# A recurrent matrix-memory layer with an MLP behind it: wider matmul tiles, wider fillers and a new hand-written order on one Trainium2 core

## The chip, the core and the metric

One NeuronCore of a Trainium2 chip runs the whole program. It has a matrix engine (TensorE, PE in the profile, with its weight loads shown apart as PEld), a vector engine (VectorE, DVE), an activation engine (ScalarE, ACT), a general engine (GpSimd, POOL), and a queue that only issues transfers here (SyncE, SP). The metric is the time on the device of one execution, in microseconds (us); lower is better.

## The reference, cut to what matters

```python
# B=4 batches, H=8 heads, S=768 steps, D=40
for t in range(S):                                   # per batch and head
    m_new = max(f[t] + m, i[t])
    f_s, i_s = exp(f[t] + m - m_new), exp(i[t] - m_new);  m = m_new
    C = f_s * C + i_s * outer(v[t], k[t])            # 40 x 40 memory
    n = f_s * n + i_s * k[t]
    y[t] = sigmoid(o[t]) * (C @ q[t]) / max(abs(n @ q[t]), 1)
x  = y, heads side by side                           # (B, S, 320)
xn = (x - mean(x)) / sqrt(var(x) + 1e-6) * g_ln
out = x + max(xn @ w_ch1, 0) @ w_ch2                 # 320 -> 1280 -> 320
```

## The kernel before, in words

**Steps.** The sequence is cut into 6 chunks of 128 rows; a chunk of one batch is a step, so there are 24 steps, numbered `st`, four to a chunk. Two steps side by side make a pair `p` (12 of them), and the MLP works on pairs. In a step, `S` makes the scores of all heads (keys against queries), `ex` makes the decay weights with exponentials, `P` multiplies scores by weights, `int` adds what the memory of earlier chunks gives (it has matmuls from step 4 on), `pv` multiplies by the values, `km`/`kv` make the update of the memory and `sd`/`st` apply it. `n1` to `n3`, `sq` and `np` normalise the row, `T`, `xh`, `xl` transpose it and split it into a high and a low part. `G`/`sel` and `eg`/`qm` bring in the decays of later chunks from DRAM; in chunk 0 (steps 0 to 3) `gx` makes them with matmuls. The pieces that begin with `g` (`gm`, `gg`, `gate`, `gu`, `gta`, `gca`, ...) are the gates of a chunk: scans on VectorE, short rows on GpSimd, two transposes.

**MLP.** `m1.p.f.i` is 8 matmuls of 256 columns (high and low parts of weights and rows), `hh`/`hl` apply the ReLU and split the result, `m2.p.f.j` is 6 matmuls of 320 columns, `ob` adds the input row, `out` stores it. A pair has ten `m1` and ten `m2`.

**Weights.** They come as 64-bit floats, in 11 chunks (`wl.0` to `wl.10`, through 4 buffers), and the kernel turns them into a high and a low 32-bit part: `cA` (ScalarE, absolute value), `cX` (clamp from below, GpSimd), `cT.0` to `cT.2` (VectorE, bit operations), `cH` (ScalarE), `cL` (GpSimd), and four copies `cR`. The first pair needs all of them.

**Order.** Nothing is planned at run time: the string `ORDER` (lines 40 to 129) lists every piece, and each engine, and SP for the transfers, takes its instructions in that order. `@` gives the banks of the matmuls' memory. `fill.n` is a matmul whose result nobody reads. On TensorE every recorded matmul has a weight load in front; a product of 32-bit floats makes two of such pairs (a transpose one). So `S` and `int` make 64 recorded instructions, `pv` 128, `kv` 64, `m1` 16, `m2` 12, `T` 6, `gx` 36, and `fill.128` 2.

The lines that are spoken of later are 363 to 373 (`S`), 413 to 425 (`kv`), 445 to 457 (`pv`), 614 to 617 (`cX`, with the strings `CX` in line 35 and `BUFS` in line 37), 620 to 634 (`cT`), 683 to 691 (`ini`) and 693 to 695 (`fill`).

Of the kernel before, what the change touches and what calls it, by code (L numbers as in the profile page):

```python
# [47 lines left out]
gate.1 fill.128 fill.128 ex.1.0 fill.128 fill.128 fill.128 fill.128 fill.128 gu.1 gst.1 fill.128 fill.128 fill.128
fill.128 fill.128 fill.128 fill.128 fill.128 fill.128 fill.128 fill.128 fill.128 fill.128 gex.1 S.0@4@5 cH.0 gse.1
gm.2 wl.3 fill.128 ex.1.1 gta.1@7 cL.0 cR.0 fill.128 fill.128 P.0.0 fill.128 fill.128 fill.128 fill.128 cR.1 fill.128  # L50
fill.128 fill.128 fill.128 fill.128 fill.128 fill.128 P.0.1 fill.128 fill.128 sig.0 S.1@4@6 gca.1 gr.1 km.1 cR.3
fill.128 cR.2 gtr.1@7 km.0 fill.128 P.1.1 wl.4 kv.1@5 cA.1 fill.128 gg.2 P.1.0 pv.0 st.1 gcr.1 kv.0@6 n1.0 pv.1 st.0
n2.0 cX.1 S.2@4@5 n3.0 ld.4 fill.128 gx.2@0@6 cA.2 cT.1.0 n1.1 fill.128 sq.0 T.0@7 cT.1.1 cX.2 fill.128 fill.128
fill.128 fill.128 ex.2.0 fill.128 fill.128 fill.128 fill.128 fill.128 fill.128 n2.1 fill.128 fill.128 np.0 fill.128
fill.128 fill.128 fill.128 cT.2.0 gx.3@1@2 tok.2 ex.2.1 P.2.0 fill.128 cT.2.1 int.3@3@4 fill.128 fill.128 fill.128
fill.128 km.3 sig.1 fill.128 fill.128 fill.128 fill.128 fill.128 fill.128 fill.128 fill.128 fill.128 fill.128 P.2.1
ex.3.0 km.2 kv.3@0 fill.128 cT.1.2 int.2@5@6 pv.2 G.4 ex.3.1 cT.2.2 eg.2 kv.2@1 fill.128 fill.128 fill.128 fill.128
fill.128 n1.2 fill.128 fill.128 fill.128 G.5 fill.128 n3.1 fill.128 cH.2 fill.128 fill.128 fill.128 fill.128 fill.128
fill.128 fill.128 fill.128 fill.128 fill.128 fill.128 fill.128 fill.128 cH.1 fill.128 fill.128 cL.2 fill.128 fill.128
fill.128 fill.128 fill.128 fill.128 ld.5 fill.128 fill.128 xh.0 n2.2 T.1@2 st.2 fill.128 gate.2 S.3@5@6 st.3 xl.0  # L60
gst.2 xh.1 cL.1 cA.3 fill.128 n3.2 fill.128 fill.128 fill.128 fill.128 fill.128 fill.128 fill.128 sq.1 fill.128
fill.128 fill.128 fill.128 fill.128 fill.128 fill.128 gex.2 fill.128 fill.128 fill.128 fill.128 cX.3 wl.5 fill.128
fill.128 fill.128 fill.128 fill.128 fill.128 P.3.1 wl.6 T.2@7 sq.2 np.1 fill.128 fill.128 gse.2 fill.128 fill.128 cA.4
P.3.0 fill.128 fill.128 fill.128 fill.128 fill.128 fill.128 fill.128 np.2 fill.128 fill.128 fill.128 cT.3.0 xh.2 pv.3
xl.1 cX.4 fill.128 ld.6 S.4@0@1 cT.3.1 gu.2 G.6 fill.128 cT.4.0 m1.0.0.0@6 cT.3.2 cT.4.1 fill.128 cH.3 m1.0.0.1 eg.3
cL.3 n1.3 sig.2 gta.2@5 cT.4.2 fill.128 fill.128 fill.128 fill.128 fill.128 fill.128 fill.128 fill.128 hh.0.0 fill.128
fill.128 fill.128 n2.3 km.4 m1.0.1.0@2 wl.7 cH.4 xl.2 km.5 gr.2 n3.3 kv.4@3 tok.3 fill.128 cL.4 kv.5@7 m1.0.1.1 hl.0.0
sq.3 fill.128 gca.2 T.3@4 sel.4 wl.8 gm.3 hh.0.1 m2.0.0.0@6 xh.3 hl.0.1 sel.5 m2.0.0.1@5 ex.4.1 xl.3 m2.0.1.1 np.3
ex.4.0 P.4.1 S.5@2@4 qm.4 ex.5.0 P.4.0 fill.128 gtr.2@1 fill.128 qm.5 cA.5 m2.0.1.0 P.5.0 ex.5.1 gcr.2 m1.1.0.0@0 cX.5
P.5.1 gg.3 int.4@1@2 cA.6 G.7 cT.5.0 fill.128 pv.4 cT.5.1 fill.128 cX.6 m1.1.0.1 sd.4 cT.5.2 ld.8 cT.6.0 cH.5  # L70
m1.1.1.0@4 st.4 hh.1.0 cT.6.1 cL.5 m1.1.1.1 ld.7 n1.4 cT.6.2 sel.6 m1.0.2.0@3 wl.9 hh.1.1 n2.4 cH.6 m1.0.2.1 hl.1.1
qm.6 ex.6.0 n3.4 int.5@1@2 cL.6 cA.7 pv.5 hh.0.2 sd.5 hl.1.0 m1.1.2.0@4 sq.4 st.5 ex.6.1 cX.7 wl.10 hl.0.2 np.4
m2.1.0.0@7 cT.7.0 n1.5 ld.9 sig.3 km.6 cT.7.1 m2.0.2.0 km.7 n2.5 kv.6@0 cT.7.2 kv.7@3 n3.5 m2.0.2.1 cH.7 cA.8 cL.7
S.6@1@2 eg.4 gate.3 sq.5 gst.3 gex.3 sel.7 m2.1.1.0 gse.3 P.6.0 P.6.1 cX.8 m1.0.3.0@1 ex.7.0 np.5 cT.8.0 m1.0.3.1
ex.7.1 cT.8.1 G.8 gu.3 tok.4 m2.1.0.1@2 hh.0.3 cT.8.2 m2.1.1.1 qm.7 hl.0.3 cH.8 gm.4 m1.1.2.1 cA.9 cL.8 m1.1.3.0@1
hh.1.2 hl.1.2 m1.1.3.1 cA.10 cX.9 cX.10 m2.0.3.0 cT.9.0 hh.1.3 cT.9.1 gg.4 m2.0.3.1 cT.10.0 cT.9.2 m2.1.2.1 cT.10.1
cH.9 m2.1.2.0 cL.9 hl.1.3 gta.3@4 cT.10.2 gr.3 m2.1.3.0 G.9 sel.8 gca.3 gate.4 cH.10 m1.0.4.0@1 gst.4 gex.4 gu.4
ex.8.0 gse.4 m1.0.4.1 ex.8.1 m1.1.4.0@4 cL.10 gm.5 m1.1.4.1 hh.0.4 ld.11 sig.4 hl.0.4 m2.1.3.1 km.9 hh.1.4 sel.9
hl.1.4 T.4@1 m2.0.4.0 xh.4 km.8 ex.9.1 xl.4 m2.0.4.1 gg.5 ob.0.0 ex.9.0 S.7@1@4 ob.0.1 out.0.0 out.0.1 int.6@5@6
gate.5 pv.6 P.7.0 gex.5 gst.5 qm.8 gse.5 sd.6 m2.1.4.1 P.7.1 G.11 n1.6 st.6 S.8@1@4 n2.6 ob.1.1 n3.6 int.7@5@6 out.1.1  # L80
pv.7 ld.10 qm.9 T.5@0 sd.7 sq.6 P.8.1 eg.6 T.6@2 m2.1.4.0 xh.5 np.6 st.7 xh.6 P.8.0 sel.11 int.8@3@4 xl.6 pv.8 ob.1.0
ex.11.0 n1.7 kv.9@1 out.1.0 xl.5 kv.8@2 ex.11.1 gtr.3@7 sd.8 m1.2.1.0@0 gu.5 n2.7 st.8 tok.5 n3.7 m1.2.1.1 m1.2.3.0@5
# [676 lines left out]
```

## Time and profile before

| | us |
|---|---|
| median of 3 runs | 371.09 |
| lowest, highest | 367.81, 372.40 |
| the execution that was profiled, its own time | 370.03 |
| its span, from the first to the last instruction | 368.3 |
| TensorE busy in it (91%) | 334.1 |
| VectorE busy (56%) | 208.1 |
| ScalarE busy (39%) | 144.8 |
| GpSimd busy (37%) | 136.1 |

What the trace says is of the one profiled execution; its own time lies 1.7 us above its span, and 1.06 us under the median of the runs. A busy share is a mean over stages with different limits, so a stretch has to be read by itself. The page of the profile names, for every idle moment, what ended it; "issue" stands where the profile shows nothing that the engine waited for.

### The profile page before, as it was taken

How to read it: one execution, taken by the hardware profiler on the slowest of the kernel's cores; microseconds unless marked ns; L12 is line 12 of the kernel's file. 1: busy time of each engine (PE TensorE's matmuls, PEld its weight loads, DVE VectorE, ACT ScalarE, POOL GpSimd, SP SyncE). 2: the span in 40 equal slices, each digit the busy share in tenths (PEclk: the TensorE clock that was granted, in tenths of full speed). 3: DMA queues.
4: the chain of work that ended last, by engine and by line, in shares of the span. 5: the costliest groups of instructions: out<-in, count | busy, mean ns of one | idle time of the engine just before them, and what ended most of it. 6: DMA issues, size and time to landing. Idle time of an engine off the chain costs nothing.

```text
span 368.3 us, 12884 instructions
## 1 busy us (share of the span) xinstructions
PE 334.1 (91%) x5664; PEld 317.5 (86%) x5664; DVE 208.1 (56%) x475; ACT 144.8 (39%) x374; POOL 136.1 (37%) x169
## 2 busy tenths in 40 slices
...
GB/s 198 302 263 261 226 236 329 81 183 131 136 52 185 248 165 89 118 219 74 159 245 128 117 189 24 28 117 175 189 262 70 17 4 0 2 72 3 0 2 71
DMA packets 15956, 49.42 MB, mean 134 GB/s; under 512 B 1916, under 2 KB 5532, under 8 KB 15900
## 3 DMA queue, kind: packets, MB, share of 16 engines
...
q8 instruction: 44, 0.72, 0.8%
q14 instruction: 12, 0.10, 0.1%
HBM read 43.84 MB, written 4.10 MB: 130 GB/s over the span
## 4 chain that ended last, share of the span: by engine, by line
PE 75%; DVE 8%; issue 7%; POOL 6%; ACT 2%; DMA 1%; SPq 0%; POOLq 0%; DVEq 0%; ACTq 0%
PE banks L550 29%; PE banks L577 9%; PE banks L579 8%; PE banks L578 8%; PE banks L371 5%; PE banks L694 4%; PE banks L454 4%; POOL wt L617 3%; PE banks L407 2%; PE banks L421 2%; PE banks L355 1%; PE banks L516 1%; ACT w L340 1%; DVE y L486 1%; DVE wt L627 1%
## 5 line engine op out<-in xcount | busy, mean ns | idle before, releaser
L562 DVE SCALAR_TENSOR_TENSOR hl<-banks,hh 128x512 fp32r<-128x512 f32 x60 | 41.1, 687 | 77.7 <-ACT hh L555 77.7
L577 PE MATMUL banks<-w2h,hh 128*128 128x320 f32 x240 | 76.8, 320 | 2.2 <-DVE state L442 2.0
L579 PE MATMUL banks<-w2h,hl 128*128 128x320 f32 x240 | 75.0, 313 | 2.2 <-DVE hl L562 2.2
L578 PE MATMUL banks<-w2l,hh 128*128 128x320 f32 x240 | 74.8, 312 | 0.0
L555 ACT ACTIVATE hh<-banks 128x512 fp32r<-128x512 f32 x60 | 35.6, 596 | 92.0 <-PE banks L550 87.4
L550 PE MATMUL banks<-xh,w1h 128*128 128x256 f32 x360 | 66.8, 295 | 0.5 <-DVE w L378 0.4
L550 PE MATMUL banks<-xh,w1l 128*128 128x256 f32 x360 | 64.5, 289 | 2.8 <-issue 2.5
L550 PEld LDWEIGHTS banks<-xh,w1l 128*128 128x128 f32 x360 | 53.2, 196 | 3.3 <-issue 2.7
L550 PEld LDWEIGHTS banks<-xh,w1h 128*128 128x128 f32 x360 | 54.0, 197 | 1.6 <-ACT gg L288 0.7
L340 ACT ACTIVATE w<-w,ar_sb 128x128 f32<-128x128 f32 x160 | 48.9, 390 | 5.4 <-POOL w L329 4.7
L550 PE MATMUL banks<-xl,w1h 128*128 128x256 f32 x240 | 49.1, 287 | 0.0
L577 PEld LDWEIGHTS banks<-w2h,hh 128*128 128x128 f32 x240 | 45.4, 189 | 3.3 <-DVE state L442 2.2
L579 PEld LDWEIGHTS banks<-w2h,hl 128*128 128x128 f32 x240 | 45.5, 190 | 2.5 <-DVE hl L562 2.5
L578 PEld LDWEIGHTS banks<-w2l,hh 128*128 128x128 f32 x240 | 45.6, 190 | 0.1
L384 POOL TENSOR_TENSOR qe<-qk,eg 104x512 f32<-104x512 f32 x20 | 26.4, 1329 | 40.7 <-PE banks L407 19.5
L378 DVE TENSOR_TENSOR w<-banks,w 128x512 f32<-128x512 f32 x48 | 31.5, 684 | 16.7 <-ACT w L340 7.3
L504 POOL TENSOR_SCALAR rs<-rs 128x1 f32<-128x1 f32 x24 | 6.0, 252 | 88.8 <-ACT junk L498 87.8
L550 PEld LDWEIGHTS banks<-xl,w1h 128*128 128x128 f32 x240 | 38.0, 194 | 0.0
L498 ACT ACTIVATE junk<-y,sum 128x320 bf16<-128x320 f32 x24 | 13.5, 561 | 41.6 <-DVE sum L489 41.5
L454 PEld LDWEIGHTS banks<-tok,w 128*32 128x32 f32 x1536 | 17.4, 112 | 12.6 <-issue 11.8
L329 POOL TENSOR_SCALAR_AFFINE_SELECT w<-w 128x1024 f32<-128x1024 f32 x20 | 23.7, 1190 | 9.5 <-DMA w<-gsc 7.2
L371 PE MATMUL banks<-qk 40*64 40x128 f32 x768 | 27.0, 281 | 0.1
...
## 6 DMA issues: line engine op xcount, KB each, us to landing
...
```

The costliest lines, as they stand in the source:

```text
L329: nc.gpsimd.affine_select(out=w, in_=w, pattern=[[0, H], [1, C]], compare_op=ALU.is_ge, fill=NEG, base=0, channel_multiplier=-1)
L340: nc.scalar.activation(out=w[:, h], in_=ps[:, hh], func=AF.Exp, bias=ar_sb[:, c, 0, b * H + h:b * H + h + 1])
L371: nc.tensor.matmul(s_t[st, z][m, g], t[r, 1, g, m], t[r, 0, g], start=True, stop=True, skip_group_check=True)
L378: nc.vector.tensor_tensor(out=w, in0=s_t.pop((st, half)), in1=w, op=ALU.mult)
L384: nc.gpsimd.tensor_tensor(out=t, in0=qk_t[st][:, 0], in1=eg_t[p][:, j], op=ALU.mult)
L454: nc.tensor.matmul(Y[m, h], w[:, h, m], tok_t[p][:, j, h * VA:(h + 1) * VA], start=(c == 0), stop=(c == 0 or g == 3), skip_group_check=True,)
L550: nc.tensor.matmul(ps[:, i], a, x, start=(n == 0), stop=(n == len(ops) - 1))
L555: nc.scalar.activation(out=t, in_=h1_t[p, f], func=AF.Relu)
L562: nc.vector.scalar_tensor_tensor(out=l.rearrange("p a t -> p (a t)"), in0=ps.rearrange("p a t -> p (a t)"), scalar=0.0, in1=t.rearrange("p ...
L577: nc.tensor.matmul(ps, t[:, i, sl], w2h[:, ff], start=(ff == 0), stop=False)
L578: nc.tensor.matmul(ps, t[:, i, sl], w2l[:, ff], start=False, stop=False)
L579: nc.tensor.matmul(ps, l[:, i, sl], w2h[:, ff], start=False, stop=(ff == KF - 1))
```

## The change

Four edits. `S`, `kv` and `pv` of the first four steps (`NE = 4`) use tiles twice as wide (128 instead of 64 columns of weights in `S`, 64 instead of 32 in `kv` and `pv`), so these pieces have half as many matmuls there; later steps keep theirs. The 245 fillers of 128 columns become 18 of 512 columns (`fill.512`) and 4 products of 32-bit floats on 512 columns (`fill.513`, two pairs each). The clamp `cX` of all 11 chunks goes from GpSimd to VectorE. And `ORDER` is written anew: four chunks of weights (3, 2, 0, 1) are loaded and turned ahead of the first scores, the steps of chunk 0 run as 1, 0, 2, 3, and of the later steps `int`, `kv` and `pv` lie further apart, with `m1` and `m2` between. The buffers of `w` and `qk` become 5 each. The diff, with the order cut to its head on both sides and to the surroundings of steps 14 (before) and 10 (after):

```diff
 UMIN = 2.0 ** -15
 
 GP = 4
-CX = "ppppppppppp"
+NE = 4
+CX = "ddddddddddd"
 CL = "ppppppppppp"
-BUFS = {'y': 7, 'xt': 2, 'ht': 4, 'wraw': 4, 'w': 4, 'qk': 4}
+BUFS = {'y': 7, 'xt': 2, 'ht': 4, 'wraw': 4, 'w': 5, 'qk': 5}
 
 ORDER = """
-int.0@0@1 ini id g0 int.1@2@3 wl.0 gin ld.1 fill.128 fill.128 cst fill.128 fill.128 fill.128 fill.128 fill.128
-fill.128 fill.128 ld.0 fill.128 fill.128 fill.128 fill.128 fill.128 fill.128 fill.128 tok.0 fill.128 fill.128 fill.128
-fill.128 gm.0 fill.128 fill.128 fill.128 wl.1 fill.128 fill.128 fill.128 fill.128 fill.128 fill.128 gg.0 fill.128
-fill.128 fill.128 fill.128 fill.128 fill.128 fill.128 fill.128 fill.128 fill.128 fill.128 fill.128 fill.128 gate.0
...
-S.14@2@3 gr.4 gca.4 ob.4.1 ex.17.1 S.16@4@6 out.4.1 P.14.0 ld.18 ex.17.0 int.15@0@1 P.14.1 m2.4.2.0 sd.15 ex.16.0
-m2.4.3.0 ex.16.1 P.16.0 m2.4.4.0 P.16.1 S.15@2@7 ob.4.0 eg.8 S.17@3@4 P.15.1 out.4.0 int.14@5@6 P.15.0 pv.14 P.17.0
-sd.14 pv.15 P.17.1 kv.15@7 n1.14 kv.14@2 n2.14 m1.6.0.0@3 st.15 qm.16 n3.14 gtr.4@4 m1.5.1.0@5 qm.17 n1.15 sq.14 eg.9
-gcr.4 int.16@6@7 n2.15 st.14 km.16 int.17@0@1 n3.15 pv.17 np.14 kv.16@4 km.17 sd.17 pv.16 sq.15 ld.19 n1.17 sd.16
...
+int.1@0@1 ini id g0 int.0@2@3 gin wl.3 wl.2 fill.513 gm.0 gg.0 ld.1 gate.0 wl.0 gu.0 gx.1@4@5 wl.1 gm.1 cA.3 gg.1 cX.3
+gta.0@6 fill.512 cT.3.0 fill.512 gr.0 gca.0 cT.3.1 gtr.0@6 ex.1.0 fill.512 fill.512 fill.512 gcr.0 gate.1 cT.3.2
+ex.1.1 gu.1 gst.1 gx.2@4@6 cA.2 gm.2 gta.1@5 fill.513 gex.1 ex.2.0 gse.1 gca.1 gg.2 cX.2 fill.512 cT.2.0 ex.2.1
+gx.0@4@5 cT.2.1 tok.0 ld.0 cA.0 cT.2.2 fill.513 cH.3 cX.0 fill.512 cT.0.0 ex.0.0 cL.3 fill.512 ld.2 fill.512 cT.0.1
+cH.2 S.1@4@6 cT.0.2 ex.0.1 cL.2 fill.512 fill.512 P.1.0 fill.512 ld.3 cA.1 P.1.1 gx.3@4@5 cH.0 cX.1 cT.1.0 km.1 sig.0
+cT.1.1 pv.1 km.0 ex.3.0 gate.2 cst cT.1.2 gu.2 gst.2 kv.1@6 gr.1 n1.1 kv.0@4 gex.2 n2.1 G.5 cH.1 gse.2 S.0@0@1 cL.0
+gm.3 st.1 st.0 ex.3.1 S.2@4@6 tok.1 P.0.0 cL.1 P.0.1 gta.2@0 cR.0 gtr.1@5 gr.2 gca.2 P.2.1 pv.0 gg.3 n3.1 ld.5 S.3@0@1
+cR.2 fill.512 P.2.0 sq.1 sel.5 gtr.2@6 gate.3 fill.513 P.3.1 gex.3 gst.3 gu.3 ex.5.0 gse.3 fill.512 gcr.2 n1.0
+fill.512 P.3.0 fill.512 G.4 ex.5.1 n2.0 int.2@0@1 np.1 gta.3@4 ld.4 fill.512 gm.4 int.3@2@3 fill.512 gr.3 gca.3 gg.4
+gcr.1 n3.0 gtr.3@6 pv.3 sig.1 pv.2 gcr.3 km.2 sq.0 gate.4 n1.3 gst.4 gex.4 km.3 T.0@4 n2.3 eg.2 T.1@5 n1.2 kv.2@6 gu.4
+xh.0 n2.2 gse.4 xh.1 xl.0 kv.3@2 st.2 S.5@0@3 xl.1 st.3 np.0 gta.4@1 gm.5 sel.4 m1.0.0.0@6 wl.4 gr.4 P.5.0 n3.2
+m1.0.0.1 gg.5 ex.4.0 S.4@2@4 wl.5 ex.4.1 P.5.1 gtr.4@5 gca.4 n3.3 hh.0.0 m1.0.1.0@0 qm.5 wl.7 sq.2 T.2@3 m1.0.1.1 qm.4
+hl.0.0 sq.3 P.4.0 xh.2 T.3@1 hh.0.1 m2.0.0.1@6 gate.5 np.2 xh.3 gcr.4 gst.5 xl.2 cA.4 m2.0.0.0@7 cR.1 np.3 xl.3 tok.2
+gex.5 gu.5 int.4@2@3 gse.5 cX.4 cA.5 cR.3 m1.1.0.0@5 cT.4.0 ld.6 hl.0.1 m1.1.0.1 cT.4.1 m1.1.1.0@1 sd.4 hh.1.0 cT.4.2
+m1.1.1.1 hl.1.0 cH.4 P.4.1 gta.5@0 cA.7 m2.1.0.1@5 cL.4 cX.5 hh.1.1 gca.5 cX.7 m2.1.0.0@4 cT.5.0 wl.9 hl.1.1 m2.0.1.1
+wl.6 cT.5.1 sig.2 km.4 m2.1.1.1 cT.7.0 km.5 cT.5.2 m2.0.1.0 cT.7.1 cH.5 pv.4 cT.7.2 cL.5 kv.4@0 cH.7 n1.4 m2.1.1.0
+st.4 cL.7 n2.4 eg.3 cA.9 m1.1.2.0@1 n3.4 m1.0.2.0@0 wl.8 cX.9 sq.4 cT.9.0 m1.0.2.1 cT.9.1 np.4 cA.6 m1.0.3.0@2 hh.0.2
+cT.9.2 cX.6 m1.1.2.1 cH.9 cT.6.0 cL.9 hl.0.2 m1.0.3.1 hh.1.2 cT.6.1 wl.10 m1.1.3.0@3 hh.0.3 hl.1.2 cA.8 m1.1.3.1 tok.3
+hl.0.3 cT.6.2 m1.0.4.0@0 hh.1.3 cX.8 cH.6 m1.1.4.0@1 cT.8.0 G.6 hl.1.3 cL.6 m1.0.4.1 ld.7 cT.8.1 cA.10 m1.1.4.1 cT.8.2
+m2.0.2.1 cX.10 cH.8 cT.10.0 m2.1.2.1 cT.10.1 cL.8 m2.0.2.0 cT.10.2 ld.8 m2.1.2.0 sig.3 km.7 cH.10 T.4@2 m2.1.3.1 xh.4
...
+hl.4.3 m2.4.2.1 S.15@0@2 int.10@4@5 P.15.1 pv.10 sd.10 P.15.0 m1.4.4.0@1 n1.10 st.10 m1.4.4.1 n2.10 n3.10 int.11@2@3
+pv.11 qm.12 sd.11 sq.10 m2.4.0.0@0 st.11 n1.11 n2.11 qm.13 m2.4.1.0 hh.4.4 n3.11 S.14@4@5 np.10 hl.4.4 sq.11
+int.13@2@3 pv.13 np.11 sd.13 kv.13@7 n1.13 T.10@1 st.13 m2.4.3.1 n2.13 xh.10 n3.13 m2.4.2.0 T.11@7 int.12@2@3 xl.10
...
 """
@@ -166,7 +149,7 @@
     g_sb = const.tile([128, DM], F32)
     junk = const.tile([128, DM], BF16)
     ones_sb = const.tile([GR, 1], F32)
-    wu_bf = const.tile([128, 128], BF16)
+    wu_sb = const.tile([128, 512], F32)
     mh_sb = const.tile([128, 1], F32)
     ar_sb = const.tile([128, NC, 2, 32], F32)
     w1h = const.tile([128, 3, FF], F32R)
@@ -364,10 +347,11 @@
         t = qk_t[st]
         for z in range(2):
             s_t[st, z] = banks[:, at[z]].rearrange("p (h t) -> p h t", t=C)
+        n = C if st < NE else 64
         for g in range(4):
-            for j in range(2):
+            for j in range(0, C, n):
                 for z in range(2):
-                    r, m = slice(64 * z, 64 * z + D), slice(64 * j, 64 * j + 64)
+                    r, m = slice(64 * z, 64 * z + D), slice(j, j + n)
                     nc.tensor.matmul(
                         s_t[st, z][m, g], t[r, 1, g, m], t[r, 0, g], start=True, stop=True, skip_group_check=True
                     )
@@ -414,12 +398,13 @@
         p, j = divmod(st, 2)
         ps = banks[:104, at, :4 * VA].rearrange("p (g d) -> p g d", g=4)
         kf = kps[st % 2]
+        n = 64 if st < NE else 32
         for g in range(4):
-            for z in range(4):
-                h = g + 4 * (z // 2)
-                e = h * D + 32 * (z % 2)
+            for z in range(0, C, n):
+                h = g + 4 * (z // 64)
+                e = h * D + z % 64
                 nc.tensor.matmul(
-                    banks[32 * z:32 * z + 32, at, g * VA:(g + 1) * VA], kf[:, e:e + 32],
+                    banks[z:z + n, at, g * VA:(g + 1) * VA], kf[:, e:e + n],
                     tok_t[p][:, j, h * VA:(h + 1) * VA], start=True, stop=True, skip_group_check=True,
                 )
         kv_t[st] = ps
@@ -446,11 +431,12 @@
         c, b = divmod(st, B)
         p, j = divmod(st, 2)
         Y, w = Y_t[st], W_t[st]
+        n = 64 if st < NE else 32
         for g in range(4):
             for z in range(2):
                 h = 4 * z + g
-                for x in range(4):
-                    m = slice(32 * x, 32 * x + 32)
+                for x in range(0, C, n):
+                    m = slice(x, x + n)
                     nc.tensor.matmul(
                         Y[m, h], w[:, h, m], tok_t[p][:, j, h * VA:(h + 1) * VA],
                         start=(c == 0), stop=(c == 0 or g == 3), skip_group_check=True,
@@ -681,7 +667,7 @@
     @piece
     def ini():
-        nc.vector.memset(wu_bf, 0.0)
+        nc.vector.memset(wu_sb, 0.0)
         nc.vector.memset(mt[0][:, 0:1], NEG)
         nc.vector.memset(ones_sb, 1.0)
         nc.vector.memset(mh_sb, -0.5)
@@ -691,7 +677,8 @@
             nc.gpsimd.memset(t[:, DM:], 0.0)
     @piece
     def fill(n):
-        nc.tensor.matmul(banks[:, 7, 512 - n:], id_bf, wu_bf[:, :n], start=not busy, stop=False, skip_group_check=True)
+        a, x = (id_sb, wu_sb) if n > 512 else (id_bf, wu_sb.bitcast(BF16)[:, :n])
+        nc.tensor.matmul(banks[:, 7, 0:x.shape[1]], a, x, start=not busy, stop=False, skip_group_check=True)
         busy.append(n)
     with tc.manual_schedule():
```

## Rows read from the trace of the kernel before

**Rows 1.** The page's first part: busy time and share, and instructions recorded, by engine.

```profile
PE 334.1 (91%) x5664; PEld 317.5 (86%) x5664; DVE 208.1 (56%) x475; ACT 144.8 (39%) x374; POOL 136.1 (37%) x169
```

**Rows 2.** Stretches: length, busy (count) PE PEld DVE ACT POOL, clock, transfers' share, GB/s.

```profile
0.00:20.00 20.00, 16.68 (x349) 14.31 (x350) 9.19 (x29) 10.41 (x26) 12.07 (x25) 1.00 0.91 260
20.00:53.00 33.00, 24.09 (x529) 20.10 (x514) 17.74 (x44) 12.56 (x36) 15.52 (x17) 0.79 0.96 244
53.00:102.00 49.00, 42.90 (x625) 39.20 (x626) 44.06 (x73) 26.62 (x65) 43.15 (x40) 0.92 0.56 170
102.00:368.30 266.30, 250.40 (x4182) 243.89 (x4181) 137.07 (x332) 95.24 (x248) 65.35 (x88) 0.98 0.34 105
```

**Rows 3.** The chain that ended last: start, length, what; TensorE's pauses.

```profile
20.16 3.92 issue
...
149.28 1.66 issue
...
176.84 2.04 issue
...
204.34 2.69 issue
...
213.82 1.87 issue
...
256.64 2.38 issue
...
293.30 0.83 issue
```

**Rows 4.** Stretches again: single blocks, and four blocks between two pauses.

```profile
39.05:46.15 7.10, 6.77 (x126) 6.11 (x127) 4.80 (x16) 3.00 (x9) 2.49 (x3) 0.76 0.91 225
147.68:150.94 3.26, 1.60 (x144) 1.43 (x135) 1.92 (x6) 0.00 (x0) 0.72 (x1) 1.00 0.46 135
175.42:178.88 3.46, 1.42 (x129) 1.29 (x130) 1.86 (x8) 0.00 (x0) 1.41 (x2) 1.00 0.31 117
150.94:178.88 27.94, 25.70 (x511) 25.16 (x512) 14.71 (x37) 5.91 (x12) 8.41 (x11) 1.00 0.44 137
```

**Rows 5.** The page's third part: one transfer queue, its packets, MB and share.

```profile
q8 instruction: 44, 0.72, 0.8%
```

**Rows 6.** Line 617 (clamp) and line 623 (next operation): count, duration ns min/median/max.

```profile
L617 POOL TENSOR_SCALAR wt<-wt x11: 1474/1795/2113, 6.8 to 96.0; 128x640 f32<-128x640 f32 x6, 128x512 f32<-128x512 f32 x5
L623 DVE TENSOR_SCALAR wt<-wt x11: 418/494/836, 9.0 to 97.9; 128x640 int32<-128x640 int32 x6, 128x512 int32<-128x512 int32 x5
```

**Rows 7.** VectorE in order of time, 91 to 104 us: start, us, operation.

```profile
91.66 4.23 DVE L251 TENSOR_TENSOR_SCAN mt<-gin,mt 32x128 f32<-32x128 f32 x1
...
100.76 1.41 DVE L631 SCALAR_TENSOR_TENSOR wraw<-wraw,wt 128x640 int32<-128x640 int32 x1
...
103.48 0.47 DVE L251 TENSOR_TENSOR_SCAN mt<-gin,mt 32x128 f32<-32x128 f32 x1
```

**Rows 8.** The chain again: prices of TensorE's pieces, later part.

```profile
212.30 0.74 PE banks L454 x64
...
248.41 1.91 PE banks L371 x64
...
250.32 0.91 PE banks L407 x64
...
254.39 0.44 PE banks L421 x32
...
349.56 4.76 PE banks L550 x40
...
364.13 0.15 PE banks L577
```

**Rows 9.** Groups by line and shape: count, busy us, mean ns, idle before; fillers.

```profile
L694 PE MATMUL banks<-wu_bf,id_bf 128*128 128x128 bf16 x245 | 23.7, 255 | 3.0 <-POOL id_bf L675 2.1 <-issue 0.3 <-DVE ar_sb L312 0.3
```

**Rows 10.** A stretch of the later part with two dips of the clock.

```profile
178.00:212.00 34.00, 30.42 (x614) 29.27 (x617) 19.64 (x53) 15.51 (x47) 10.28 (x13) 0.90 0.61 169
```

More of the change, by code (lines that the diff above doesn't have):

```diff
@@ L48 @@
[L48 to L82, printed above, removed]
```

96 lines of the change are left out of this document (49 added, 47 removed).

## The prediction

> **What bounds the kernel now.** I began with the page's first part: TensorE is busy 91% of the span, no other engine above 56% [rows 1]. A share over stages says little, so I cut the span where VectorE ends `cT.10.2`, the last bit operation on the last chunk of weights (1.41 us from 100.76) [rows 7]. The three parts then have three limits [rows 2]. From 102 us on TensorE is busy 250.40 of 266.30 us: 15.9 us idle. From 53 to 102 us VectorE is busy 44.06 of 49 us (90%) and GpSimd 43.15. From 20 to 53 us nobody is full: VectorE 17.74 of 33, TensorE 24.09 at a granted clock of 0.79, beside transfers at 0.96 of the time.
>
> Then the chain of waits, for those 15.9 us: after 140 us it has six pauses called "issue", in which TensorE waits for nothing that the profile shows: 1.66 + 2.04 + 2.69 + 1.87 + 2.38 + 0.83 = 11.47 us, and an early one of 3.92 us at 20.16 [rows 3]. What they are shows when instructions are counted. Between the ends of the pauses at 150.94 and 178.88 us, 511 matmuls and 512 weight loads are recorded, 1,023, or four times 256; the last of these blocks (175.42 to 178.88) has 259, and the one that ends with the pause at 150.94 has 279, as loads near an edge fall to one side or the other [rows 4]. One queue carries instructions: 44 packets, 0.72 MB [rows 5], so 16 KB each, and 2 x 5,664 recorded instructions over 44 are 257 a packet [rows 1]. So TensorE pauses at the end of a block of 256 instructions whose successor has not arrived. The two late blocks took 3.26 and 3.46 us for 1.60 and 1.42 us of work; beside heavy transfers one took 7.10 us [rows 4]. A refill therefore sets a least time per block: 3.3 to 3.5 us late, about 7 us early.
>
> The Trainium skill (Runtime: NRT & Kernel Launch, section "Instruction fetch mechanics") also has blocks of 256 instructions, but holds that their fetch is hidden, because the sequencer dispatches more slowly than it is filled. By that rule the pauses are no refills and fewer instructions give nothing back; the pauses at multiples of 256 speak against it, and it stands as rival 3.
>
> **The change part by part.** *Instruction count.* By the order's words, fillers go from 490 instructions to 52, and the wide tiles save 32 (`S`), 32 (`kv`) and 64 (`pv`) in each of four steps, 512 in all. Up to `cT.10.2` the old order issues 2,952, the new one 1,590: 11.5 against 6.2 blocks. At 7.1 us that is 82 us, most of what before needs to get there, against 44 us, which is less than VectorE's work in the same part. So the refill leaves the early path.
>
> *Late blocks.* I cut both orders into blocks of 256 and priced them by [rows 8]: `m1` 4.76 / 5 = 0.95 us, `m2` 6 x 0.15 = 0.90, `S` 0.96, `int` 0.46, `pv` 0.74, `kv` 0.44. The old order has eight blocks of 1.5 to 2.4 us of work after `cT.10.2`, where steps lie back to back. In the new one the shortest (most of `pv.10`, two `m1`, `int.11`, part of `pv.11`) has 3.3 us and no other is under 3.7. At 3.46 us a refill nearly all 11.47 us go; I take 0 left, 2 us if refills are slower there.
>
> *Wide tiles.* No row shows them. They make half as many matmuls, each with twice the columns of weights and the same rows to multiply. Between half and twice the time of a piece, a step costs from 1.1 us less to 2.1 more (0.96 + 0.44 + 0.74), 8.6 us at most for four. I take 0, since it lies under VectorE's work: TensorE's pieces up to `cT.10.2` are 20 `m1`, 11 `m2`, 6 `S`, 5 `pv`, 5 `kv`, 1 `int`, some 41 us, and under 10 us of transposes and `gx`.
>
> *Fillers.* 245 were busy 23.7 us [rows 9], 0.10 each, so 18 of four times the columns cost up to 7.0 us; the four on 32-bit floats lie between 0.4 and 1.7 each. That makes 9 to 14 us, or 60 to 65 us of TensorE in a part of 86. Cover: VectorE's work. If the clock were 0.79 there, as from 20 to 53 us [rows 2], 65 us would last 82, so the cover is thin.
>
> *The clamp.* GpSimd loses 11 x 1.795 = 19.7 us. On VectorE the nearest row is the next operation on the same tile, 418 to 836 ns, median 494 [rows 6]: 11 x 0.494 = 5.4 us (4.6 to 9.2). Against this, VectorE's operations stretch beside GpSimd: a scan of 32 x 128 took 4.23 us at 91.66 and 0.47 at 103.48 [rows 7]. Up to 102 us GpSimd works 12.07 + 15.52 + 43.15 = 70.7 us [rows 2] and loses over a quarter; I credit VectorE 4 us, about one such scan (0 to 8). The Trainium skill (SBUF — State Buffer, section "SBUF: two separate sides") calls the port pair of the two engines an exclusive lock that also a one-input VectorE operation in its two-port mode takes. By that rule each clamp would hold GpSimd off, for 5.4 us in all; the trace shows the lock only from the other side, in the 4.23 us.
>
> *The new place of the weights.* Chunks 3, 2, 0, 1 are turned ahead of the first scores, when VectorE was idle for 10.8 of 20 us. Its first pieces have to wait for transfers, so of those 20 us I fill 13 (9.2 as before; 20 would need data that has not landed). By `cT.10.2` the new order has asked for two `ld`, one `tok`, two `G` and one `eg` fewer than the old. The old moved 0.26 x 20 + 0.244 x 33 + 0.17 x 49 = 21.6 MB (MB per us, times us) by then; at 250 GB/s the smaller load needs less than 86 us. SP issues in order, so a transfer that waits for a buffer holds those behind it, as before.
>
> *The sum, against the profiled execution.* VectorE up to `cT.10.2` in before: 9.19 + 17.74 + 44.06 = 71.0 us, and 0.2 to 102.2. The new order has two `P` and one step's `n1` to `n3`, `sd`, `st` less there and one `gm`, two `gate` and five small copies more: even, within 2 us. With the clamps +5.4 and the relief -4 it is 72.6. Point reached: 20 + (72.6 - 13) / 0.90 = 86.2 us, where before stood at 102.2. Rest in before: 368.3 - 102.2 = 266.1; less the pauses 11.5; less the clock, 0.90 over 34 us [rows 10], 3.4; that is 251.2. At that point TensorE has three `m2`, one `S`, one `int`, one `pv`, three `kv` less behind it (6.2 us) and four `m1` more (3.8): + 2.4, so 253.6. Span 86.2 + 253.6 = 339.8, and 1.7 around it, as before (370.03 - 368.3): 341 us, beside 370.03 for the profiled execution. The median of the runs, 371.09, is 1.06 us above that; I leave the forecast at 341.
>
> Ends: VectorE at 65.8 us (71.2 - 2 + 4.6 - 8) without idle time after 20 us gives 72.8 + 251.2 + 1.7 = 326; at 82.4 us (71.2 + 2 + 9.2) with 9.2 in the first 20, 101.3 + 253.6 + 2 + 1.7 = 359.
>
> **Rivals.**
>
> *1. The early part is no faster* (clock, or transfers held up in SP's order take the refill's place): 102.2 + 253.6 + 1.7 = 357.5. For it: transfers at 0.91 and 0.96 in the first 53 us, the thin cover of 65 us at 0.79. Against it: fewer bytes, and half the instructions.
>
> *2. No gain to speak of.* Beside rival 1, the weights hold up the first step: three more chunks, 1.7 MB, go ahead of `tok.0`, 6.9 us at 250 GB/s: 364. It needs both.
>
> *3. The pauses are no refills* but belong to the bursts of small matmuls: the late 11.5 us stay, 341 + 11.5 = 352.5. For it: all pauses lie in `pv` or `kv`. Against it: the multiples of 256.
>
> *4. Slower.* Without 245 fillers TensorE stays at 1.2 GHz up to `cT.10.2`: its 60 to 65 us become 120 to 130, and 253.6 + 1.7 on top is 375 to 385. It is slower than before from 115 us on (370.0 - 255.3). Against it: the clock was at 0.92 from 53 to 102 us with TensorE busy 42.90 of 49, and a TensorE that becomes the limit is busy all the time.
>
> **How the numbers follow.** Forecast 0.64 (331 to 351); still faster, as VectorE is never idle, 0.04; rival 1 0.18; rival 3 0.06; rival 2 0.05; rival 4 0.03. A measurement of this kernel can tell 2% from no change, 7.4 us: faster means under 362.6. So faster 0.64 + 0.04 + 0.18 + 0.06 = 0.92, same 0.05, slower 0.03. The range 328 to 358 takes in rivals 1 and 3 and leaves out 2, 4, most of the fastest case and the edge of rival 1, near 2 in 10.
>
> **What would show it.** Right: fewer packets in the instruction queue (about 41 for 10,378 instructions); no "issue" of over 1 us after `cT.10.2`; that word near 86 us; line 617 on VectorE near 0.5 us; a span behind it near 254 us, with TensorE idle under 5 us. Wrong: `cT.10.2` after 95 us, with VectorE waiting for DMA, or a clock under 0.8 for long; pauses where no block is short; `pv` of steps 0 to 3 far over 0.74 us.

## The result, and the profile after

The changed kernel takes 350.83 us (median; 347.84 to 356.30), against 371.12 for the kernel before beside it: ratio 0.944, 95% interval [0.935, 0.953], 5.6% faster. The forecast was 341 with a range of 328 to 358, so the direction and the range held and the point was 10 us too low. The profiled execution took 352.78 us with a span of 351.0, 17.3 us under the span of before. Some executions of a kernel take over 1.5% longer than its fastest one: the ratios here leave them out, the medians and ranges do not, and the profiled executions of old_wide_fill, new_fill_early and new_shift64 below (376.11, 354.80 and 354.29 us) are of that kind.

The page's parts one and three (busy time by engine; the queue that carries instructions), against [rows 1, 5]:

```profile
PE 329.6 (94%) x5189; PEld 305.2 (87%) x5189; DVE 208.5 (59%) x486; ACT 145.5 (41%) x374; POOL 116.1 (33%) x158
...
q8 instruction: 41, 0.67, 0.8%
```

The last bit operation on the weights, VectorE in order of time, against 100.76 + 1.41 in [rows 7]; behind it the stretches cut there, and the slow part of the early stretch (20.00 to 37.20), against [rows 2] (length, busy (count) of PE, PEld, DVE, ACT, POOL, clock, transfers' share, GB/s):

```profile
82.26 1.16 DVE L617 SCALAR_TENSOR_TENSOR wraw<-wraw,wt 128x640 int32<-128x640 int32 x1
```

```profile
0.00:20.00 20.00, 15.90 (x91) 8.25 (x92) 14.93 (x33) 12.40 (x34) 10.91 (x24) 1.00 0.85 259
20.00:53.00 33.00, 31.99 (x397) 26.23 (x398) 25.81 (x72) 19.87 (x57) 22.98 (x36) 0.74 0.61 178
53.00:83.40 30.40, 29.10 (x333) 27.84 (x332) 29.67 (x49) 13.14 (x21) 13.33 (x11) 1.00 0.77 233
83.40:351.00 267.60, 252.65 (x4374) 242.84 (x4373) 138.05 (x335) 100.11 (x263) 68.85 (x88) 0.99 0.39 117
20.00:37.20 17.20, 17.03 (x168) 13.65 (x168) 11.00 (x30) 9.38 (x28) 10.43 (x15) 0.50 0.64 172
```

So the whole gain lies ahead of the last bit operation: it ends at 83.4 us instead of 102.2, 18.8 sooner. The rest takes 267.6 us where before took 266.1: it gained nothing, and was forecast to gain 12.5.

The chain of waits shows what stayed in the rest (start, length, what), against [rows 3]:

```profile
88.08 0.77 issue
...
101.72 12.05 DMA eg<-esc
113.99 1.27 POOL qe L368
115.62 0.56 POOL rs L491
116.18 1.06 POOL w L312
117.57 2.15 ACT w L323 x7
119.74 0.70 DVE w L362
120.49 0.67 PE banks L391 x30
...
177.23 0.82 issue
...
208.50 1.52 issue
...
259.93 1.93 issue
```

Four pauses of the old kind stand in it (5.04 us), and two that are not on the chain: TensorE is empty for 0.70 us before 147.87 and for 0.33 before 230.72. That makes 6.1 us. TensorE in order of time, with the idle time before each group and what ended it:

```profile
147.87 0.31 PE L564 MATMUL banks<-w2l,hh 128*128 128x320 f32 x1 [0.70 <-issue]
...
149.00 0.44 PE L502 MATMUL banks<-id_sb,xn 128*128 128x128 f32 x2 [0.67 <-DVE xn L477]
...
230.72 0.31 PE L564 MATMUL banks<-w2l,hh 128*128 128x320 f32 x1 [0.33 <-issue]
```

The 0.67 us in the middle is an ordinary wait for VectorE's `xn`, and no pause of this kind. The six pauses and 8.0 us of the expectations below count it as one, leave out the one at 230.72, and run from the start of the last instruction before a pause to the start of the next.

A new wait stands at 117.5: decays (`eg`) land late, and `int.7` waits for a bank through `qm`, `sel`, `ex` and `P` (1.84 + 0.81 us).

### The profile page after: what moved, and what is told of

It reads as the page before. It is cut to its first block, busy times and chain, and to the rows that moved or that the text cites. A ratio compares the mean times of both kernels' runs of the same rounds, so it can differ in the third digit from the quotient of the medians.

```text
span 351.0 us, 11943 instructions
## 1 busy us (share of the span) xinstructions
PE 329.6 (94%) x5189; PEld 305.2 (87%) x5189; DVE 208.5 (59%) x486; ACT 145.5 (41%) x374; POOL 116.1 (33%) x158
## 4 chain that ended last, share of the span: by engine, by line
PE 72%; DVE 16%; issue 4%; DMA 4%; ACT 1%; SPq 1%; POOL 1%; DVEq 0%; POOLq 0%
PE banks L536 25%; PE banks L563 9%; PE banks L565 8%; PE banks L564 8%; PE banks L355 6%; PE banks L440 5%; DMA eg<-esc 3%; PE banks L391 3%; DVE wt L613 3%; DVE wraw L617 2%; PE banks L406 2%; PE banks L338 1%; PE banks L681 1%; PE banks L502 1%; DVE wt L603 1%
## 5 line engine op out<-in xcount | busy, mean ns | idle before, releaser
L541 ACT ACTIVATE hh<-banks 128x512 fp32r<-128x512 f32 x60 | 35.5, 595 | 83.4 <-PE banks L536 76.4
L536 PE MATMUL banks<-xh,w1h 128*128 128x256 f32 x360 | 64.8, 289 | 0.0
L536 PE MATMUL banks<-xh,w1l 128*128 128x256 f32 x360 | 63.1, 285 | 0.0
L536 PEld LDWEIGHTS banks<-xh,w1h 128*128 128x128 f32 x360 | 52.9, 192 | 0.8 <-issue 0.3
L536 PEld LDWEIGHTS banks<-xh,w1l 128*128 128x128 f32 x360 | 51.9, 191 | 0.0
L312 POOL TENSOR_SCALAR_AFFINE_SELECT w<-w 128x1024 f32<-128x1024 f32 x20 | 21.9, 1097 | 46.6 <-DMA w<-gsc 34.2
L355 PE MATMUL banks<-qk 40*64 40x128 f32 (+1 forms) x704 | 28.2, 285 | 0.0
L355 PEld LDWEIGHTS banks<-qk 40*64 40x64 f32 (+1 forms) x704 | 23.5, 147 | 2.4 <-issue 0.8
L490 POOL TENSOR_SCALAR rs<-rs 128x1 f32<-128x1 f32 x24 | 5.1, 211 | 53.0 <-ACT junk L484 52.0
```

Source lines behind the costliest of these rows:

```text
L312: nc.gpsimd.affine_select(out=w, in_=w, pattern=[[0, H], [1, C]], compare_op=ALU.is_ge, fill=NEG, base=0, channel_multiplier=-1)
L355: nc.tensor.matmul(s_t[st, z][m, g], t[r, 1, g, m], t[r, 0, g], start=True, stop=True, skip_group_check=True)
L536: nc.tensor.matmul(ps[:, i], a, x, start=(n == 0), stop=(n == len(ops) - 1))
L541: nc.scalar.activation(out=t, in_=h1_t[p, f], func=AF.Relu)
```

## The experiments

Each kernel ran beside the kernel before on the same chip, and its ratio is to that. The kernel before had medians of 371 to 375 us in these groups of runs, so ratios compare better than medians. "Last bit" is the end of the last bit operation in the profiled execution, "rest" its span behind it (both from the trace, VectorE in order of time).

| kernel | median (range) us | ratio to before, 95% | last bit | rest |
|---|---|---|---|---|
| before | 371.09 (367.81–372.40) | | 102.2 | 266.1 |
| old_wide | 364.42 (361.91–367.91) | 0.974 [0.964, 0.984] | 92.8 | 269.7 |
| old_wide_fill | 373.86 (368.87–378.62) | 1.001 [0.995, 1.006] | 99.2 | 275.1 |
| old_clampv | 369.66 (365.81–373.97) | 0.995 [0.989, 1.001] | 101.2 | 268.0 |
| order_alone | 358.32 (356.67–361.19) | 0.962 [0.953, 0.970] | 94.4 | 263.6 |
| **after** | 350.83 (347.84–356.30) | 0.944 [0.935, 0.953] | 83.4 | 267.6 |
| new_clampp | 360.91 (359.10–362.63) | 0.975 [0.962, 0.988] | 91.0 | 266.3 |
| new_narrow | 349.21 (346.39–349.73) | 0.931 [0.924, 0.938] | 79.3 | 265.2 |
| new_fill_early | 350.29 (349.27–354.80) | 0.946 [0.931, 0.960] | 81.8 | 271.2 |
| new_out_late | 352.46 (348.76–356.62) | 0.945 [0.920, 0.971] | 83.0 | 266.0 |
| new_wide_all | 354.23 (351.68–357.23) | 0.955 [0.939, 0.971] | 84.2 | 267.8 |
| new_shift64 | 353.35 (346.98–355.80) | not taken | 82.1 | 270.4 |
| **new_wide_s** | **343.26** (341.98–344.81) | 0.917 [0.910, 0.925] | 83.0 | 258.4 |
| new_wide_s_out | 349.67 (346.64–350.39) | 0.933 [0.925, 0.940] | 82.2 | 266.3 |

The old kernels stand on the kernel before, the new ones on the kernel after.

### The parts of the change, one by one

**old_wide**: the old order with the wide tiles of steps 0 to 3.

```diff
+NE = 4
...
-            for j in range(2):
+            for j in range(0, C, n):
...
-                for x in range(4):
-                    m = slice(32 * x, 32 * x + 32)
+                for x in range(0, C, n):
+                    m = slice(x, x + n)
```

> The old order with the wide tiles of steps 0 to 3 and nothing else. Refill theory (early in the old order TensorE waits for blocks of 256 instructions, about 7 us each beside heavy transfers): 512 instructions, two blocks, less among the first 1,700, so 8 to 14 us off if every one of those blocks is held up, and the pauses before 53 us shrink or go; 357 to 364 us. Rival, work theory (the early part is set by when the weights are turned, and the number of instructions does not matter): within 2 us of 371. Both: the six pauses after 140 us stay, about 11.5 us.

The stretch from 20 to 53 us (columns as above) and one wide `pv`, TensorE in order of time:

```profile
20.00:53.00 33.00, 28.48 (x516) 24.72 (x513) 27.74 (x62) 17.81 (x49) 24.49 (x28) 1.00 1.00 262
```

```profile
29.65 1.13 PE L458 MATMUL banks<-tok,w 128*64 128x41 f32 x32
```

VectorE does 27.74 us of work there instead of 17.74 [rows 2], and the last bit operation ends 9.4 us sooner. With 512 instructions fewer the early refills no longer set the pace: that was the early bound, at a price of 1.13 us for a wide `pv` (a narrow one takes 0.81, in the kernel after at 86.12 us). The granted clock rose with it, from 0.79 to 1.00, so the run does not tell the pauses' own time from what the lower clock cost. The late pauses stayed: 512 is exactly two blocks and moves no later boundary.

**old_wide_fill**: as old_wide, with every fourth filler only (62 of 245).

```diff
-int.0@0@1 ini id g0 int.1@2@3 wl.0 gin ld.1 fill.128 fill.128 cst fill.128 fill.128 fill.128 fill.128 fill.128
...
+int.0@0@1 ini id g0 int.1@2@3 wl.0 gin ld.1 fill.128 cst ...
```

> The old order with the wide tiles, and of its 245 fillers only every fourth kept (62): 878 instructions less than before, 3.4 blocks, all of them among the first 1,700. Refill theory: a further 3 to 8 us off the kernel with wide tiles alone, 350 to 358 us. Work theory: 371. Clock theory (the fillers are needed to hold TensorE at 2.4 GHz): slower than the kernel with wide tiles alone by 3 us or more, with a lower granted clock in the first 60 us.

`S` and `pv` in order of time:

```profile
24.62 2.08 PE L358 MATMUL banks<-qk 40*128 40x128 f32 x16
...
35.14 1.92 PE L443 MATMUL banks<-tok,w 128*64 128x41 f32 x32
```

Both run at half speed (1.16 and 1.13 us in old_wide); the clock itself has no record in this trace before 47 us. The ratio is 1.001 against 0.974: the 183 fillers less lose all that the wide tiles had won. Without the fillers' work TensorE was not at 2.4 GHz here, so the mechanism of rival 4 exists. The two profiled executions lie 11.8 us apart, 6.4 of them ahead of the last bit operation. Behind it (rest 275.1 against 269.7) 878 instructions fewer than in before have moved the boundaries, and TensorE's pauses come to 15.6 us against 11.8; whether that part stands in every execution is not shown.

**old_clampv**: the clamp alone.

```diff
-CX = "ppppppppppp"
+CX = "ddddddddddd"
```

> The old order with only the clamp of the weights on VectorE. My sum for it: VectorE gets 5.4 us, and its operations are stretched less beside GpSimd by about 4 us, so the 53 to 102 us part is about even: 368 to 373 us. Rival (GpSimd, busy 43 of 49 us there, is the true limit of that part): 8 to 12 us off, 359 to 363. The single clamp: 0.42 to 0.84 us. A long scan as the 4.23 us one at 91.66 us should be gone.

Even, within what can be measured. Both halves of the sum can be read: the 11 clamps take 5.2 us of VectorE, its longest scan of the kind that took 4.23 us takes 0.48, and its whole work up to the last bit operation stays at 71.2 us (71.15 before). **new_clampp** is the same edit undone in the new order:

> The new kernel with the clamp back on GpSimd. By the sum, the clamps cost VectorE 5.4 us and save 4 by less stretch, but in the new order the chain of a weight chunk becomes 1.3 us longer for each of 11 and VectorE is 97% busy from 40 to 83 us, waiting in order for GpSimd: the last bit operation ends 3 to 7 us after 83.4, 353 to 357 us. Rival (VectorE is the limit and gets 5.4 us back): 2 to 4 us off, 346 to 348.

10 us slower by the medians, more than the 3 to 7 expected. The difference shows in VectorE's group behind the clamp (first bit operation; busy, mean ns | idle before it and what ended that), first of the kernel before, then of new_clampp:

```profile
L623 DVE TENSOR_SCALAR wt<-wt 128x640 int32<-128x640 int32 (+1 forms) x11 | 6.2, 562 | 2.8 <-POOL wt L617 2.7
```

```profile
L609 DVE TENSOR_SCALAR wt<-wt 128x640 int32<-128x640 int32 (+1 forms) x11 | 10.2, 931 | 14.0 <-POOL wt L603 14.0
```

In the old order VectorE has other work while GpSimd clamps and waits 2.7 us; in the new one, with the chunks back to back, it would wait 14.0. The clamp on VectorE costs 6.8 us there (group below, of the kernel after) and takes that wait away.

```profile
L603 DVE TENSOR_SCALAR wt<-wt 128x640 f32<-128x640 f32 (+1 forms) x11 | 6.8, 617 | 0.3 <-ACT wt L596 0.3
```

The stretch up to the last bit operation, of the kernel after and then of new_clampp, shows VectorE's work and idle time as a whole:

```profile
0.00:83.40 83.40, 76.98 (x816) 62.31 (x816) 70.41 (x152) 45.42 (x111) 47.23 (x70) 0.90 0.72 218
```

```profile
0.00:91.02 91.02, 76.76 (x814) 60.22 (x816) 69.14 (x141) 45.28 (x111) 67.64 (x81) 0.98 0.65 199
```

With the clamp VectorE works 1.3 us more, so its other operations take 5.5 us less in all beside a GpSimd that works 47.23 us instead of 67.64. It is idle for 13.0 us instead of 21.9.

**order_alone**: the new order with narrow tiles, each `fill.512` as four and each `fill.513` as sixteen `fill.128`, the clamp on GpSimd.

```diff
-NE = 4
-CX = "ddddddddddd"
+NE = 0
+CX = "ppppppppppp"
...
```

> The new order with the three other edits undone: narrow tiles in all steps, fillers of 128 columns (four for each of 512 columns, sixteen for each product of 32-bit floats), the clamp on GpSimd. It has 11,110 instructions, 2,320 of them up to the last bit operation on the weights, 9.1 blocks. Refill theory: 9.1 blocks of 7 us are 64 us, still under the 83 us that the new kernel needs to that point, so the order alone keeps most of the gain: 351 to 358 us. Rival (the fewer and wider instructions make the gain): 362 to 371 us.

The order alone is worth 3.8%, two thirds of the change. "Order" takes in here the two more buffers, which stay, and 136 fillers instead of 245. **new_narrow** is the kernel after without wide tiles:

```diff
-NE = 4
+NE = 0
```

> The kernel after without wide tiles in the first four steps (512 instructions, two blocks, more up to the last bit operation). If VectorE alone sets the early pace and the wide tiles give nothing inside the new order: last bit operation at 83 to 85 us, no early refill pause over 1 us, 349 to 353. If the wide tiles keep the refill off the early path (2 blocks x 3.5 to 7 us): one or two refill pauses of 2 to 5 us between 20 and 50 us, last bit operation at 87 to 91, 354 to 358.

The last bit operation ends 4.1 us sooner than with wide tiles, and the median is not worse. The stretch from 20 to 53 us, and TensorE's longest pause in it:

```profile
20.00:53.00 33.00, 28.38 (x693) 24.41 (x694) 29.71 (x77) 19.36 (x58) 22.92 (x34) 0.92 0.70 212
```

```profile
29.14 0.56 PE L440 MATMUL banks<-tok,w 128*32 128x41 f32 x36 [1.50 <-issue]
```

From 20 us to the last bit operation the chain has no "issue" over 1.01 us, and the pause of 1.50 us is not on it. So in the new order with few fillers the early refills no longer set the pace, and the wide tiles win nothing there. The clock is higher too, 0.92 against 0.74 in the kernel after; how much of the 4.1 us is the price of wide tiles and how much the clock, no run tells.

### What sets the early pace in the new order

**new_fill_early**: 18 more fillers, two after each of seven pieces and four ahead of `gx.3`, where TensorE waits 2.36 us.

```diff
+fill.513 fill.513 fill.512 fill.512
 gx.3@4@5
...
 S.0@0@1
+fill.512 fill.512
...
```

> The new kernel with 18 more fillers (2 products of 32-bit floats and 16 of 512 columns) ahead of and between the pieces from gx.3 to S.3, where TensorE was busy 19.77 of 20 us at a granted clock of 0.57. Clock theory (the early part of the new kernel loses time because pieces of few rows and narrow tiles do not keep TensorE at 2.4 GHz, and only then VectorE sets the pace): the stretch at 1.2 GHz from 20.1 to 37.2 us goes or shrinks to under 7 us, pv.3 starts 3 to 7 us earlier than at 38.9, the last bit operation on the weights ends 2 to 6 us before 83.4; 344 to 349 us. Rival (VectorE and the transfers set the pace anyway): within 2 us of the new kernel, or slower by the fillers' own 5 us.

The stretch from 20 to 40 us, first of the kernel after, then of this one:

```profile
20.00:40.00 20.00, 19.77 (x213) 15.45 (x214) 13.27 (x38) 10.99 (x32) 12.41 (x19) 0.57 0.66 182
```

```profile
20.00:40.00 20.00, 17.96 (x272) 12.48 (x274) 16.32 (x44) 11.57 (x34) 14.85 (x21) 1.00 0.64 182
```

The clock is whole, VectorE does 3 us more there, and the last bit operation comes only 1.6 us sooner: VectorE has little room left behind (29.67 of 30.4 us from 53 us on in the kernel after). The time is that of the kernel after, so the clock in this stretch is a small term, as the rival had it.

### What stayed in the late part

**new_out_late**: the stores `out` go up to 60 words later in the order.

```diff
-... S.6@2@3 out.1.1 tok.4 S.8@4@5 ...
+... S.6@2@3 tok.4 S.8@4@5 ... out.1.1
...
```

> The new kernel with the stores of pairs 0 to 8 issued up to 60 places later in the order, behind the loads that stood behind them in the transfer queue. Queue theory (SyncE waits at a store for its result, the loads behind it start late and all at once, which makes POOL wait for eg.4 up to 113.8 us, TensorE stop for 2.7 us at 117.5 us, and refills slow beside the burst): the stop at 117.5 us goes, and of the 8.0 us of refill pauses after 83 us some 2 to 4 us; 343 to 348 us. Rival (the loads are needed late, so it is hidden but for that one stop): 2 to 3 us off, 348 to 349. The buffers of y are freed later, which could stop n1 and cost as much.

```profile
100.00:120.00 20.00, 20.00 (x424) 18.86 (x424) 11.70 (x30) 10.43 (x31) 4.64 (x5) 1.00 0.67 193
```

The stop at 117.5 us is gone (TensorE 20.00 of 20 busy), but the refill pauses are 2.43 us at 173.0 and 3.63 at 255.5 now, and nothing is won.

**new_wide_all**: wide tiles in all 24 steps.

```diff
-NE = 4
+NE = 24
```

> The new kernel with the wide tiles in all 24 steps. Ten blocks of instructions less, so the pauses for refills (8.0 us) and the two dips of the clock behind the longest of them (3.4 us) should go. Price theory (measured in steps 0 to 3 at full clock: pv 1.13 against 0.81 us, kv 0.66 against 0.50, S 1.16 against 1.10, some 0.5 us a step): 20 steps cost 10 to 11 us, so it ends even, 349 to 353 us. Rival (the price is not paid where TensorE is full, since loads hide behind other matmuls): 339 to 343 us.

```profile
84.20:352.00 267.80, 261.36 (x3237) 252.31 (x3237) 135.17 (x334) 99.81 (x263) 68.14 (x88) 0.99 0.40 116
```

The pauses vanish and TensorE is busy 8.7 us longer (252.65 in the kernel after): even.

**new_shift64**: 32 fillers of 64 columns in the 2.36 us in which TensorE waits ahead of `gx.3`; all later boundaries fall 64 instructions earlier.

```diff
+fill.64 fill.64 fill.64 fill.64
...
 gx.3@4@5
```

> The kernel after, with 32 fillers of 64 columns (64 instructions, about 1 to 1.5 us of TensorE) put where TensorE waits 2.36 us for VectorE at 17.8 us, so that every later block boundary falls 64 instructions earlier in the stream; all else is as before. Theory (the pauses belong to where boundaries fall): each of the six pauses changes by over 0.3 us or moves to other pieces, and the time comes out anywhere from 347 to 356. Rival (pauses belong to the dense pieces themselves): the same pauses before the same pieces, within 0.3 us each, and the time within 1 us of the kernel after.

```profile
146.31 2.38 issue
...
178.38 3.03 issue
```

The pauses at 208.5 and 259.9 us are gone and those near 146 and 178 have grown, so where boundaries fall decides which piece is hit; the sum hardly changes (6.0 us). The pauses stay where they were in the count of instructions. From the start to the pause near 147 us, first of the kernel after, then of this one:

```profile
0.00:147.17 147.17, 135.23 (x1994) 117.41 (x1995) 106.62 (x237) 75.71 (x195) 70.13 (x97) 0.94 0.66 193
```

```profile
0.00:146.31 146.31, 133.19 (x1992) 117.64 (x1995) 105.30 (x233) 73.12 (x187) 68.61 (x95) 0.92 0.65 190
```

TensorE has started 3,989 and 3,987 matmuls and weight loads by then, though 64 of the second kernel's are new fillers. So it stops some 64 instructions earlier in its work, in `kv` instead of `m2`: the count decides, not the piece. The times spread over 9 us, so only the trace is read.

**new_wide_s**: `S` wide in all steps, `kv` and `pv` wide in the first four only.

```diff
-        n = C if st < NE else 64
+        n = C
```

> The kernel after, with the wide tile of S (128 columns of weights) in all 24 steps instead of the first four; kv and pv stay narrow from step 4 on. S is the densest piece: 64 instructions in 1.10 us narrow, 32 in 1.16 wide (the run with everything wide showed both), so 20 steps save 640 instructions (2.5 blocks of 256) for 20 x 0.06 = 1.2 us. Theory (the pauses left in the kernel after are refills of blocks with too little work, and the dense pieces make them): the 8.0 us of pauses behind the last bit operation fall to 2 to 4, the clock dips once at most, and the time is 344 to 348. Rival (density of S does not decide, only where the boundaries happen to fall): the pauses move and their sum stays at 6 to 10 us; 349 to 354. A page that shows fewer packets in the instruction queue (38 or 39 instead of 41) and pauses unchanged at the same pieces would speak against refills altogether.

The groups of `S` (mean ns behind the busy time), first of the kernel after, then of this one, and this one's stretch behind the last bit operation:

```profile
L355 PE MATMUL banks<-qk 40*64 40x128 f32 x640 | 21.1, 274 | 0.0
```

```profile
L355 PE MATMUL banks<-qk 40*128 40x128 f32 x384 | 27.8, 289 | 1.6 <-DVE mt L233 0.8 <-issue 0.8
```

```profile
83.00:341.40 258.40, 251.94 (x4085) 242.60 (x4085) 134.98 (x335) 99.94 (x263) 68.11 (x88) 0.99 0.40 121
```

A wide `S` has half the instructions for up to a tenth more time (1.09 us in the chain, against 0.96 to 1.03). The rest falls by 9.2 us, and this nearly adds up: the pauses fall from 6.1 to 0.8 us (one, at 109.3), the stop at 117.5 from 2.65 to 0.25 (why, no run shows), the 0.67 us wait for `xn` is gone, one dip of the clock stands there instead of two (1.7), and 1.2 to 2 us are paid. The kernel is faster than before and after: 343.26 us, 0.917 [0.910, 0.925], an interval clear of that of the kernel after.

**new_wide_s_out**: the same with the late stores.

```diff
-        n = C if st < NE else 64
+        n = C
...
-... S.6@2@3 out.1.1 tok.4 S.8@4@5 ...
+... S.6@2@3 tok.4 S.8@4@5 ... out.1.1
```

> The kernel before this one, with the stores also moved up to 60 words later in the order (as in the run of late stores, which took away the stop at 117.5 us). If the two gains add, 2 us under the run with wide S alone: 342 to 346. If the stop at 117.5 only hid other waits, the same as with wide S alone.

The gains don't add; 6.4 us are lost again. TensorE's pieces stand in the order of new_wide_s, but two pauses are back (chain). The second ends a block beside heavy transfers; the same 256 instructions in new_wide_s stand last, with no pause behind them:

```profile
126.09 1.99 issue
...
176.90 3.78 issue
```

```profile
172.63:180.68 8.05, 4.27 (x150) 3.86 (x138) 3.98 (x14) 1.64 (x4) 0.74 (x2) 0.93 0.96 238
```

```profile
171.81:175.87 4.06, 4.06 (x150) 3.78 (x139) 3.22 (x12) 1.64 (x4) 0.74 (x2) 1.00 0.49 199
```

The only edit between the two kernels is the place of the stores: the block took 8.05 us at a transfers' share of 0.96 and 4.06 at 0.49.

## Why the prediction was right, and where its sum was wrong

**The early part: right in size, by another split.** Forecast 86.2 us, measured 83.4. VectorE's work was 14.93 + 25.81 + 29.67 = 70.4 us (forecast 72.6), with 14.93 in the first 20 us (13). The 90% was two things: 78% from 20 to 53 us, 98% behind it. The first is the thin cover that the prediction named: TensorE had 31.99 of 33 us of work at a clock of 0.74, which is also one of its signs of being wrong (a clock under 0.8 for long). The fillers measured 6.5 + 6.1 = 12.6 us (9 to 14 forecast), and the packets 41.

**What carried it was not what the sum said.** By the last bit operation, in one profiled execution of each kernel, the 18.8 us are 7.8 from the order (order_alone), 3.4 from wide tiles and fillers together (from order_alone to new_clampp) and 7.6 from the clamp (from new_clampp to the kernel after). Fewer instructions at the early refills are worth 9.4 us in the old order (old_wide). That fits TensorE's early pauses in the kernel before, 3.92 + 2.20 + 0.30 + 2.46 us, all ahead of 53 us, and not a refill that paces the whole of 102 us, as "82 us, most of what before needs" had it. But in the new order the wide tiles gave nothing (new_narrow); the fillers alone were not tried there. The clamp was booked at 5.4 - 4 us, a small loss, and these two terms were right: 6.8 us spent, 5.5 saved on VectorE's other operations. Missing was the wait that it takes away, 14.0 us of VectorE in the new order, which left it 8.9 us less idle in all. VectorE's wait for the clamp (2.7 us in the kernel before) had to be worked out anew for an order in which no other work stands beside it.

**The total held in part by luck.** The last bit operation came 2.8 us sooner than forecast and the rest took 14.0 us longer, so two misses of opposite sign leave 11.2 us of span. The time stands at the upper end of what the forecast gave itself (331 to 351); the wider range took it in with room.

**Late blocks: the failed step.** "In the new one the shortest has 3.3 us and no other is under 3.7; I take 0 left." The rest was forecast at 253.6 us, 249.4 of work and 4.2 idle (15.9 - 11.5, less 0.2 for the cut); it measured 252.65 and 14.95. The 10.75 us of idle time more are 6.1 of refill pauses and 4.75 of new waits (2.1 where TensorE waits for `xh` right behind the last bit operation, 2.65 at 117.5), less 0.1 in small gaps. Of the 3.25 busy, two new dips of the clock make about 3.4: 3.4 us each at half speed from 211.3 and 262.5, behind the two longest pauses.

Stretches between the ends of pauses in the kernel after, then the last block ahead of four pauses, against [rows 4]:

```profile
88.85:147.87 59.02, 55.67 (x1017) 52.73 (x1017) 32.76 (x76) 26.46 (x75) 19.06 (x24) 1.00 0.63 173
147.87:178.05 30.18, 28.69 (x640) 26.90 (x639) 20.79 (x50) 12.33 (x33) 10.28 (x15) 1.00 0.56 174
178.05:210.02 31.97, 30.39 (x508) 29.12 (x509) 16.02 (x40) 11.30 (x31) 8.17 (x11) 1.00 0.31 91
210.02:261.86 51.84, 49.58 (x1018) 47.46 (x1018) 28.04 (x71) 20.61 (x55) 17.26 (x22) 0.97 0.44 128
```

```profile
86.15:88.85 2.70, 1.93 (x133) 1.75 (x131) 2.60 (x10) 1.89 (x7) 2.70 (x3) 1.00 0.02 6
173.18:178.05 4.87, 4.05 (x137) 3.70 (x129) 4.03 (x14) 2.18 (x6) 1.65 (x4) 1.00 0.54 196
204.81:210.02 5.21, 3.69 (x143) 3.34 (x136) 3.16 (x11) 1.10 (x4) 1.40 (x3) 1.00 0.77 207
258.18:261.86 3.68, 1.75 (x137) 1.59 (x130) 1.30 (x4) 0.43 (x2) 1.97 (x3) 1.00 0.02 4
```

Matmuls and loads in the four stretches are 2,034, 1,279, 1,017 and 2,036 (one that spans an edge is counted on both sides): 8, 5, 4 and 8 blocks of 256, less 14, 1, 7 and 12. So the stream holds other instructions too, 34 in these 25 blocks. I had counted the two recorded kinds alone; that the boundaries I drew were off for this reason is argued, not tried. Two things are read directly. Two of the blocks hold 1.75 and 1.93 us of work, which my cut did not have. And two with 3.69 and 4.05 us of work, long enough for a refill of 3.46 us, still ended in a pause: the block took 4.87 to 5.21 us at a transfers' share of 0.54 to 0.77. That the transfers slow a refill is what new_wide_s_out shows, with 8.05 us at 0.96 where the same block took 4.06 at 0.49. I had taken the price of quiet blocks (share 0.31 and 0.46 [rows 4]) for all.

**Rival 3** gave 352.5 us, closest to the result, by the wrong mechanism. It held that the pauses are no refills, which is what the rule of the Trainium skill amounts to (Runtime: NRT & Kernel Launch, "Instruction fetch mechanics": the fetch is hidden as the sequencer dispatches slowly). The runs speak against it: fewer instructions for the same products take the pauses away (6.1 us to 0.8 with wide `S`), moving stores alone brings them back, and 64 fillers far ahead move them to other pieces at the same count (new_shift64). **Rival 1** fell, as did **rival 2**: the last bit operation came 18.8 us sooner. **Rival 4** did not happen as a whole: TensorE ran at half its clock from 20.1 to 37.2 us only. old_wide_fill shows that its mechanism is real in the old order.
